# Leftover tokens of a top-1 MoE: the first gathered item as a ninth batch, the small item in column groups

## The chip, the cores and the metric

The kernel runs on one core of a Trainium2 chip. The metric is the device time of one execution in microseconds (us), as the median of several runs; every time below is in us unless ns is written. A core has five engines: TensorE (PE, with its weight loads shown apart as PEld), VectorE (DVE), ScalarE (ACT), GpSimd (POOL) and SyncE (SP, which here only issues DMA transfers and loads registers), and 16 DMA engines that serve all queues.

## What is computed

Sigmoid attention for 8 batches, 12 heads, 448 positions and 64 features a head feeds a mixture of 8 experts, of which each token takes one.

```python
def _attn_ref(q, k, v):
    scores = scale * np.matmul(q, k.transpose(0, 1, 3, 2)) - np.log(S)
    attn = 1.0 / (1.0 + np.exp(-scores))
    return np.matmul(attn, v)

def _moe_ref(x, w_gate, w1, w2):          # x 3584 x 768, w1 8 x 768 x 1024, w2 8 x 1024 x 768
    logits = x @ w_gate
    expert_idx = np.argmax(logits, axis=1)
    ...
    for e in range(E):
        xe = x[expert_idx == e]
        h = np.maximum(xe @ w1[e], 0.0)
        out[mask] = gate_w[mask, None] * (h @ w2[e])
```

On the inputs used, one expert holds nearly every token of a batch. What is left over, worked out from the reference, is 218 tokens of expert 7 and one token of expert 3.

## The kernel before

**Attention.** The 48 pairs of heads (g = 0 to 47, six for each batch) are read by SyncE and POOL: `load_pair` brings q and k, `load_values` (line 443, the transfer in 450) brings v. v of groups 4 to 9 comes through POOL's queue, all others through SyncE's (`V_POOL`, line 519). Scores (line 489) and weighted values (line 505) are plain fp32 matmuls on 64 by 64 tiles of the PE array; of every pair of such instructions one logical product is made.

**A batch of the MoE.** `moe` (line 194) runs for each batch the expert that most of its tokens chose, over all 448 tokens: layer 1 in line 210 (stationary: a 128 by 128 piece of w1), layer 2 in line 233. Each operand is split into a high and a low part in fp32r, and each product is made of three matmuls (high·high, high·low, low·high). `Weights` (line 135) feeds them: raw weights come by SyncE into a ring `wst` of five buffers (`load`), then ACT casts the high part (line 133) and POOL subtracts it for the low one (line 134), into rings of 3 buffers for w1 and 5 for w2 (`ahead`). The matmuls of attention and MoE are generators that are woven into each other; the order is written out by hand, and `until(n)` (line 626) lets the last batch run until n of its matmuls are left. A batch is written to the output by SyncE (line 190).

**The leftover.** Tokens that chose another expert than their batch's are noted as records (token, gate) in memory. They form items: each with one expert, and either up to 256 rows (large) or up to 128 rows (small). Counting and ordering them is done on DVE and POOL by lines 640 to 701, inside the last batch. Then two loops run with a number of passes that is only known at run time: the one of line 906 over the large items, the one of line 911 over the small. Here each is passed once. One pass, `item` (line 804), multiplies with the rows in the stationary place: 512 columns of w1 in layer 1, after which h is transposed (line 861) and split again, and 256 columns of w2 in layer 2 (all in line 815). Its positions of splits are the numbers in `AT`. `scatter` (line 768) writes the results of the item before, on POOL. The first item's rows are gathered by POOL (line 724) while the last batch runs, and its w1 is loaded and split then too (`w1h_item`, `w1l_item`).

Of the kernel before, what the change touches and what calls it, by code (L numbers as in the profile page):

```python
# [19 lines left out]
P = 128  # L20
# [5 lines left out]
def tile_sigmoid_attention_top1_moe(  # L26
# [109 lines left out]
    class Weights:  # L136
# [24 lines left out]
        def ahead(self, n):  # L161

            while True:
# [355 lines left out]
    WARM, FILL, V_POOL, K_POOL = 60, 20, 10, 12  # L519
# [90 lines left out]
    wts = Weights([(lambda b=b: regs.get(b)) for b in range(B)])  # L610
# [18 lines left out]
    for s, n in attention():  # L629
        if s >= START:  # L630
# [12 lines left out]
    AT = (  # L643
        (
            dict(zip((0, 1, 2, 3, 4, 12, 5, 6, 7, 8, 13, 14, 15, 16, 9, 10, 11, 17),
                     (38, 43, 48, 54, 60, 84, 102, 108, 114, 120, 126, 132, 138, 144, 150, 156, 162, 175))),
            (74, 90, 128, 168),
        ),
        (dict(zip((0, 1, 4, 5, 8, 9, 2, 3, 6, 7, 10, 11), (16, 20, 24, 28, 33, 42, 48, 54, 60, 66, 72, 78))), ()),
    )  # L650
    NK = NT // TL
    NI = E * NK


    xo = rest.tile([P, 2, DM], F32, name="xo")
    scr = xo.rearrange("p t f -> p (t f)")
# [8 lines left out]
    nc.gpsimd.iota(ek(1), pattern=[[NK, E], [1, NK]], base=0, channel_multiplier=0, allow_small_or_imprecise_dtypes=True)  # L665
# [5 lines left out]
    nc.vector.tensor_scalar(cut(0), cut(0), float(P), None, op0=ALU.add)  # L671
# [5 lines left out]
    ends = rest.tile([P, 2], F32, name="ends")  # L677
    nc.vector.tensor_copy(ends[:, 0:1], rank[0][:, NI - 1 : NI])
    nc.vector.tensor_add(ends[:, 1:2], ends[:, 0:1], rank[1][:, NI - 1 : NI])
    nc.vector.tensor_scalar(rank[1], rank[1], ends[:, 0:1], None, op0=ALU.add)  # L680
    for msk, cum in zip((big, few), rank):
        nc.vector.scalar_tensor_tensor(msk, cum, slot1, msk, op0=ALU.is_equal, op1=ALU.mult)
# [8 lines left out]

    ki = rest.tile([1, 2], I32, name="ki")
    nc.vector.tensor_scalar(ends[:, 0:1], ends[:, 1:2], -1.0, ends[:, 0:1], op0=ALU.add, op1=ALU.max)
# [6 lines left out]
    nc.vector.tensor_copy(li, pli[0:1, :TL])  # L700
    more(8)

    recs_v = recs.rearrange("(i t p) w -> i p t w", t=2, p=P)
    rec_s = rest.tile([P, 2, 2], U32, name="rec_s")
    rec_c = rest.tile([P, 2, 2], U32, name="rec_c")
    rec_n = rest.tile([P, 2, 2], U32, name="rec_n")
    xg = rest.tile([P, 2, DM], F32, name="xg")
    xp = xo.rearrange("p t (k f) -> p t k f", f=P)
# [3 lines left out]
    w1h = rest.tile([P, KD, DF], F32R, name="w1h_item")  # L712
    w1l = rest.tile([P, KD, DF], F32R, name="w1l_item")
# [7 lines left out]
    def get_rows(ireg, rec, nh):  # L721
        nc.sync.dma_start(rec, recs_v[bass.ds(ireg, 1)].rearrange("o p t w -> (o p) t w"))
        for t in range(nh):
            nc.gpsimd.indirect_dma_start(
                out=xg[:, t, :],
                out_offset=None,
                in_=x_tok,
                in_offset=bass.IndirectOffsetOnAxis(ap=rec[:, t, 0:1], axis=0),
                bounds_check=NT - 1,
                oob_is_err=False,  # L730
            )

    def sort_rows(nh):
        for t in range(nh):
            nc.vector.tensor_copy(
                xp[:, t].rearrange("p k (i s) -> p k i s", s=32), xg[:, t].rearrange("p (i k s) -> p k i s", i=4, s=32)
            )

    def split_rows(k2, nh):
        px = ps_x.tile([P, 512], F32, tag="px", name=f"px_{k2}")  # L740
        w = nh * P
        for kk in range(2):
            for t in range(nh):
                at = kk * w + t * P
                nc.tensor.transpose(px[:, at : at + P], xp[:, t, 2 * k2 + kk], ident)
        for kk in range(2):
            xh, xl = xrs[2 * k2 + kk]
            part = px[:, kk * w : (kk + 1) * w]
            nc.scalar.copy(xh[:, :w], part)
            nc.vector.tensor_sub(xl[:, :w], part, xh[:, :w].bitcast(F32))  # L750

    RAWS = [(wpool, "wst")] * RAWS_AHEAD
    turn = itertools.count()

    def raw_tile(name):
        pool, ring = RAWS[next(turn) % len(RAWS)]
        bufs = RAWS_AHEAD if ring == "wst" else None
        return pool.tile([P, 1024], F32, tag=ring, bufs=bufs, name=name)

    def w1_load(ereg, t):  # L760
        st = raw_tile(f"w1r_{t}")
        nc.sync.dma_start(st, w1[bass.ds(ereg, 1), t * P : (t + 1) * P, :].rearrange("e p n -> (e p) n"))
        return st

    def scatter(nh):
        puts = []
        for t in range(nh):
            put = nc.gpsimd.indirect_dma_start(
                out=out,
                out_offset=bass.IndirectOffsetOnAxis(ap=rec_s[:, t, 0:1], axis=0),  # L770
                in_=xo[:, t, :],
                in_offset=None,
                bounds_check=NT - 1,
                oob_is_err=False,
            )
            apart(put, puts)

    def no_rows():
        nc.gpsimd.iota(rec_s, pattern=[[0, 4]], base=int(BIG), channel_multiplier=0)

    no_rows()
    nc.gpsimd.memset(xg, 0.0)
    get_rows(item_reg(0), rec_c, 2)
    e0 = expert_reg(0)
    until(96)
    sort_rows(2)
    until(86)
    for k2 in range(KD // 2):
        split_rows(k2, 2)
        more(8)  # L790
    until(60)
    w1rs = [w1_load(e0, t) for t in range(3)]
    for t in range(KD):
        until(50 - 9 * t)
        part_split(w1rs[t], (w1h[:, t], w1l[:, t]), nc.vector)
        if t + 3 < KD:
            w1rs.append(w1_load(e0, t + 3))
    until(0)
    next(mo, None)
    order.close()  # L800
    RAWS = RAWS + [(hpool, f"hl{j}") for j in range(0, KF, 2)]
    ends_r = [nc.values_load(ki[0:1, a : a + 1], min_val=0, max_val=NI) for a in range(2)]

    def item(i, nh, split_at, sort_at):


        n = 0
        hooks = {}

        def at(m, f):  # L810
            hooks.setdefault(m, []).append(f)

        def mm(*a, **kw):
            nonlocal n
            nc.tensor.matmul(*a, **kw)  # L815
            n += 1
            for f in hooks.pop(n, ()):
                f()

        ereg = expert_reg(i)  # L820
        scatter(nh)
        if sort_at:
            enext = expert_reg(i + 1)
            get_rows(item_reg(i + 1), rec_n, nh)
        raws, parts = {}, {}
        todo = list(dict.fromkeys(u // 2 if u < NU else NU + u for u in split_at))

        def load():
            if todo:
                r = todo.pop(0)  # L830
                if r < NU:
                    raws[r] = raw_tile(f"w2r_{r}")
                    w2_rows(ereg, r, raws[r])
                else:
                    raws[r] = w1_load(enext, r - 2 * NU)

        def split(u):
            if u < NU:
                parts[u] = part_tiles("w2", 512, f"r_{u}")
                part_split(raws[u // 2][:, u % 2 * 512 : (u % 2 + 1) * 512], parts[u], nc.vector)  # L840
            else:
                t = u - NU
                part_split(raws[NU + u], (w1h[:, t], w1l[:, t]), nc.gpsimd if t % 2 else nc.vector)
            if u >= NU or u % 2:
                load()

        for _ in RAWS:
            load()
        for u, m in split_at.items():
            at(m, lambda u=u: split(u))  # L850
        half = DF // 2
        if sort_at:
            at(sort_at[0], lambda: sort_rows(nh))
            for k2 in range(KD // 2):
                at(sort_at[1 + k2], lambda k2=k2: split_rows(k2, nh))
        hts = {}

        def turn_h(f, h, hf):
            ph = ps_x.tile([P, 512], F32, tag="px", name=f"ph_{f}_{h}")
            for c in range(4):  # L860
# [81 lines left out]
```

## Time and profile before

| what | value |
| --- | --- |
| median of 3 runs | 869.01 (867.73 to 869.58) |
| the profiled execution: its own time | 869.31 |
| its span, from the first to the last instruction | 867.5 |
| granted clock of PE, mean | 0.993 |
| busy PE, ACT, POOL, DVE | 841.9 (97%), 388.8 (45%), 330.3 (38%), 318.1 (37%) |
| DMA | 120.61 MB, mean 139 GB/s |

The span is what the hardware profiler saw of one execution; about 1.8 of that execution's time lies outside it. Busy time of an engine is the time in which at least one of its instructions ran; PE's matmuls overlap, so their durations add up to more than the time they take, and what one costs is the distance to the next. "Idle before <- releaser" says what the engine waited for ahead of an instruction. The chain of waits goes back from the last instruction to what released it, step by step. The stretch to look at first is the end: the last batch's matmuls end near 793.9, the large item's near 838 and the small item's at 858.5.

### The profile page before, as it was taken

How to read it: one execution, taken by the hardware profiler on the slowest of the kernel's cores; microseconds unless marked ns; L12 is line 12 of the kernel's file. 1: busy time of each engine (PE TensorE's matmuls, PEld its weight loads, DVE VectorE, ACT ScalarE, POOL GpSimd, SP SyncE). 2: the span in 40 equal slices, each digit the busy share in tenths (PEclk: the TensorE clock that was granted, in tenths of full speed). 3: DMA queues.
4: the chain of work that ended last, by engine and by line, in shares of the span. 5: the costliest groups of instructions: out<-in, count | busy, mean ns of one | idle time of the engine just before them, and what ended most of it. 6: DMA issues, size and time to landing. Idle time of an engine off the chain costs nothing.

```text
span 867.5 us, 15542 instructions
## 1 busy us (share of the span) xinstructions
PE 841.9 (97%) x5642; PEld 640.1 (74%) x5642; DVE 318.1 (37%) x708; ACT 388.8 (45%) x697; POOL 330.3 (38%) x294
## 2 busy tenths in 40 slices
PE   8899999999999999999999999999999999999985
PEld 6464777777777767777777767777777789898875
DVE  2344135332363125322343134322352135435544
ACT  4567345345345445355345435255244422324533
POOL 8443332623243332624242413533242436641230
PEclk9999999999999999999999999999999999999998
DMA  9987764476556862786367753676454426545823
GB/s 152 127 177 188 168 156 91 97 183 159 102 128 140 190 142 51 169 187 149 70 144 176 166 123 80 149 166 146 88 151 108 118 65 165 157 111 152 287 73 111
DMA packets 326826, 120.61 MB, mean 139 GB/s; under 512 B 238596, under 2 KB 324052, under 8 KB 326752
## 3 DMA queue, kind: packets, MB, share of 16 engines
q1 hardware_dynamic: 320064, 113.77, 57.3%
q0 software_dynamic: 3904, 5.53, 3.0%
q8 instruction: 44, 0.72, 0.4%
q10 hardware_dynamic: 2784, 0.34, 0.4%
q14 instruction: 30, 0.25, 0.1%
HBM read 97.55 MB, written 24.64 MB: 141 GB/s over the span
## 4 chain that ended last, share of the span: by engine, by line
PE 88%; DMA 5%; SPq 2%; issue 2%; DVE 1%; ACT 1%; POOL 1%; POOLq 0%; another core or an unknown queue 0%; DVEq 0%; ACTq 0%
PE ps L233 26%; PE ps L210 26%; PE sc L489 14%; PE av L505 14%; PE ps L815 3%; PE psg L255 2%; DMA qn<-in_q_dram 2%; DMA w2r<-in_moe_w_dram 1%; SPq L437 1%; DMA vn<-in_v_dram 1%; DMA w1r<-in_moe_w_dram 1%; PE pg L372 1%; DVE w1l_item L134 1%; POOL w1l L134 0%; SPq L190 0%
## 5 line engine op out<-in xcount | busy, mean ns | idle before, releaser
L474 ACT ACTIVATE at<-sc,bias_s 128x448 f32<-128x448 f32 x336 | 188.1, 640 | 197.1 <-PE sc L489 188.8
L134 POOL TENSOR_TENSOR w2l<-wst,w2h 128x512 fp32r<-128x512 f32 x96 | 122.0, 1294 | 213.6 <-ACT w2h L133 213.5
L134 POOL TENSOR_TENSOR w1l<-wst,w1h 128x768 fp32r<-128x768 f32 x64 | 117.3, 1841 | 186.4 <-ACT w1h L133 166.3
L489 PE MATMUL sc<-qt,kt 64*64 64x448 f32 x1344 | 158.8, 547 | 3.8 <-DVE qt L458 2.1
L505 PE MATMUL av<-at,vn 64*64 64x448 f32 x1344 | 156.6, 543 | 3.8 <-DMA vn<-in_v_dram 3.8
L233 PE MATMUL ps<-hl,w2h 128*128 128x448 f32 x384 | 142.1, 370 | 0.0
L210 PE MATMUL ps<-xh,w1l 128*128 128x448 f32 x384 | 141.2, 368 | 0.8 <-POOL w1l L134 0.8
L210 PE MATMUL ps<-xh,w1h 128*128 128x448 f32 x384 | 141.3, 368 | 0.0
L210 PE MATMUL ps<-xl,w1h 128*128 128x448 f32 x384 | 141.2, 368 | 0.0
L233 PE MATMUL ps<-hh,w2h 128*128 128x448 f32 x384 | 141.1, 367 | 0.0
L233 PE MATMUL ps<-hh,w2l 128*128 128x448 f32 x384 | 140.8, 367 | 0.0
L489 PEld LDWEIGHTS sc<-qt,kt 64*64 64x64 f32 x1344 | 77.9, 191 | 62.6 <-issue 47.6
L218 DVE SCALAR_TENSOR_TENSOR hl<-ps,hh 128x448 fp32r<-128x448 f32 x64 | 40.0, 624 | 185.2 <-ACT hh L217 185.0
L505 PEld LDWEIGHTS av<-at,vn 64*64 64x64 f32 x1344 | 56.0, 133 | 67.1 <-issue 57.6
L217 ACT ACTIVATE hh<-ps 128x448 fp32r<-128x448 f32 x64 | 35.1, 549 | 137.2 <-PE ps L210 137.2
L133 ACT CAST w2h<-wst 128x512 fp32r<-128x512 f32 x96 | 57.7, 624 | 76.5 <-PE ps L233 74.9
L210 PEld LDWEIGHTS ps<-xh,w1l 128*128 128x128 f32 x384 | 72.1, 188 | 11.6 <-issue 4.6
L233 PEld LDWEIGHTS ps<-hl,w2h 128*128 128x128 f32 x384 | 74.6, 194 | 7.8 <-issue 3.9
L210 PEld LDWEIGHTS ps<-xl,w1h 128*128 128x128 f32 x384 | 72.1, 188 | 10.9 <-issue 4.9
L210 PEld LDWEIGHTS ps<-xh,w1h 128*128 128x128 f32 x384 | 72.1, 188 | 10.5 <-issue 4.8
L233 PEld LDWEIGHTS ps<-hh,w2h 128*128 128x128 f32 x384 | 74.6, 194 | 3.8
L233 PEld LDWEIGHTS ps<-hh,w2l 128*128 128x128 f32 x384 | 74.6, 194 | 3.4
(140 smaller groups left out, 759.2 us busy)
## 6 DMA issues: line engine op xcount, KB each, us to landing
wst<-in_moe_w_dram SPq DMA_DIRECT2D x64, 384.0 KB
wst<-in_moe_w_dram SPq DMA_DIRECT2D x48, 512.0 KB
x_tok<-xt SPq DMA_DIRECT2D x64, 168.0 KB
out_dram<-ob SPq DMA_DIRECT2D x96, 112.0 KB
qn<-in_q_dram SPq DMA_DIRECT2D x186, 56.0 KB
vn<-in_v_dram SPq DMA_DIRECT2D x84, 112.0 KB
kn<-in_k_dram SPq DMA_DIRECT2D x148, 56.0 KB
w1r<-in_moe_w_dram SPq DMA_DIRECT2D x12, 512.0 KB
```

The costliest lines, as they stand in the source:

```text
L133: nc.scalar.copy(hi, st)
L134: eng.tensor_tensor(lo, st, hi.bitcast(F32), op=ALU.subtract)
L210: nc.tensor.matmul(ps[:, :S], a[:, ws], b_, start=(t == 0 and n == 0), stop=(t == KD - 1 and n == 2))
L217: nc.scalar.activation(hh[:, :S], ps[:, :S], AF.Relu)
L218: nc.vector.scalar_tensor_tensor(hl[:, :S], ps[:, :S], 0.0, hh[:, :S].bitcast(F32), op0=ALU.max, op1=ALU.subtract)
L233: nc.tensor.matmul(ps[:, :S], a, b_, start=(j == 0 and n == 0), stop=(j == KF - 1 and n == 2))
L255: nc.tensor.matmul(psg[: 2 * E, :S], wgs[:, t], xch[b, t][n], start=(t == 0 and n == 0), stop=(t == KD - 1 and n == 1),)
L372: nc.tensor.transpose(pg[:, c * P : (c + 1) * P], gates[:, b, c : c + 1].broadcast_to([P, P]), ident)
L474: nc.scalar.activation(at, ps[:, :S], AF.Sigmoid, bias=bias_s, scale=SCALE)
L489: nc.tensor.matmul(ps[quarter(g, h), :S], ks, ops[g, "q"][OWN[h]], start=True, stop=True)
L505: nc.tensor.matmul(psv[g][OWN[h], :S], ops[g, "v"][rows, c, :], at[rows], start=(c == 0), stop=(c == KC - 1))
L815: nc.tensor.matmul(*a, **kw)
```

## The change

1. **v on SyncE.** `V_POOL` is gone; `load_values` uses SyncE for all groups.
2. **The first item is a ninth batch.** It always runs, as a large one. `large(wts, B)` takes its expert as the ninth entry of `Weights`, so that its weights pass through the same rings as those of the batches. In layer 1 a piece of w1 is stationary and the 256 rows move (h comes out turned the right way), in layer 2 h is stationary and 256 columns of w2 move: 144 and 144 matmuls, each of 256 columns. The rows are sorted and turned as before, at places before and in the last batch. Its results go to buffers of the output ring `ob` and are scattered at the end. `wts.low` moves the low parts of w2 from POOL to DVE from the last 50 matmuls of the last batch on.
3. **Small items have up to 32 rows** (`TS`), down from 128, and are computed in plain fp32, without splitting. `small_item` puts the 32 columns of output on one of four column groups of the array (`GRP`), adds up the four by a matmul with `fold` (four identities below one another), and does so in both layers. One such item (the second in the order of items) is woven into the ninth batch, in six pieces after matmuls 20, 36, 60, 78, 156 and 176 (`TINY`); its 14 weight pieces are loaded by SyncE, one at a time, from when 130 matmuls of the last batch are left.
4. **The loops** are still there for more items, from the second large one and from the second small one on: on these inputs neither has a pass.

The names stay; the line numbers move. The core of the diff:

```diff
@@ Weights
+        low = nc.gpsimd
...
-                    part_split(st[:, u % 2 * 512 : (u % 2 + 1) * 512], parts, nc.gpsimd)
+                    part_split(st[:, u % 2 * 512 : (u % 2 + 1) * 512], parts, self.low)
@@ load_values
-        eng = nc.sync if g < 4 or g >= V_POOL else nc.gpsimd
...
-            eng.dma_start(t[quarter(g, h)], v[b, 2 * hp + h].rearrange("(p c) d -> p c d", c=KC))
+            nc.sync.dma_start(t[quarter(g, h)], v[b, 2 * hp + h].rearrange("(p c) d -> p c d", c=KC))
@@ the batches
-    wts = Weights([(lambda b=b: regs.get(b)) for b in range(B)])
+    wts = Weights([(lambda b=b: regs.get(b)) for b in range(B + 1)])
...
-    ps_m2 = ctx.enter_context(tc.tile_pool(name="ps_m2", bufs=3, space=bass.MemoryType.PSUM))
+    ps_m2 = ctx.enter_context(tc.tile_pool(name="ps_m2", bufs=4, space=bass.MemoryType.PSUM))
@@ the items
+    def large(wts, b):
+        w0 = b * wts.PARTS
+        hts = []
+        for j in range(KF):
+            wts.ahead(w0 + (3, 4, 5, 6, 7, 9, 11, 13)[j])
+            whi, wlo = wts.parts.pop(w0 + j)
+            ps = ps_moe.tile([P, 512], F32, tag="moe", name=f"psi1_{j}")[:, :TL]
+            for t in range(KD):
+                xh, xl = xrs[t]
+                ws = slice(t * P, (t + 1) * P)
+                for n, (a, b_) in enumerate(((whi, xh), (whi, xl), (wlo, xh))):
+                    nc.tensor.matmul(ps, a[:, ws], b_, start=(t == 0 and n == 0), stop=(t == KD - 1 and n == 2))
+                    yield
...
+            nc.scalar.activation(hh, ps, AF.Relu)
+            nc.vector.scalar_tensor_tensor(hl, ps, 0.0, hh.bitcast(F32), op0=ALU.max, op1=ALU.subtract)
...
+        for d in range(ND):
+            for h in range(2):
+                ps = ps_m2.tile([P, 512], F32, tag="m2", name=f"psi2_{d}_{h}")[:, :DW]
+                for j in range(KF):
...
+                    for n, (a, b_) in enumerate(((hh, whi), (hh, wlo), (hl, whi))):
+                        nc.tensor.matmul(ps, a, b_, start=(j == 0 and n == 0), stop=(j == KF - 1 and n == 2))
+                        yield
+                    if h == 1 and j % 2:
+                        wts.ahead(w0 + KF + min(NU, 4 * d + j // 2 + 6))
+                to, gate = xo[h][:, d * DW : (d + 1) * DW], rec[:, h, 1:2].bitcast(F32)
+                nc.vector.tensor_scalar(to, ps, gate, None, op0=ALU.mult)
...
+        for h in range(2):
+            apart(scatter(xo[h], rec[:, h, 0:1]), puts)
+    GRP = [slice(c * TS, (c + 1) * TS) for c in range(4)]
+    def small_item():
+        xs = hpool.tile([P, 1024], F32, tag="hh6", name="xs")[:TS, :DM]
+        sort_rows(xs, xgs)
+        yield
...
+        for t in range(KD):
+            nc.tensor.transpose(px[:, t * TS : (t + 1) * TS], xs[:, t * P : (t + 1) * P], ident[:TS, :TS])
...
+        for n in range(2 * KD):
+            f, t = divmod(n, KD)
+            nc.tensor.matmul(
+                pss[f][GRP[n % 4], :half], xts_s[:, t * TS : (t + 1) * TS], w1s[:, t, f * half : (f + 1) * half],
+                start=(t < 4), stop=(t + 4 >= KD),
+            )
...
+        for j in range(KF):
+            nc.tensor.matmul(ph[:, j * TS : (j + 1) * TS], hp[:, j * P : (j + 1) * P], fold, start=True, stop=True)
...
+        for j in range(KF):
+            for ps, cs in zip(pss, cols):
+                nc.tensor.matmul(
+                    ps[GRP[j % 4], : cs.stop - cs.start], ht[:, j * TS : (j + 1) * TS], w2s[:, j, cs],
+                    start=(j < 4), stop=(j >= KF - 4),
+                )
...
+            nc.tensor.matmul(pf[:TS, : cs.stop - cs.start], fold, op[:, cs], start=True, stop=True)
...
+        scatter(xo[:TS, :DM], rec_s[:, 0, 0:1])
@@ the end of the program
+    get_rows(item_reg(0))
+    regs[B] = expert_reg(0)
+    first = nc.sync.value_load(ki[0:1, 0:1], min_val=1, max_val=NI)
+    small_rows(item_reg(first))
+    e_s = expert_reg(first)
...
+    for n in range(130, 90, -10):
+        until(n)
+        load_some(1)
+    xp = sort_large()
     for k2 in range(KD // 2):
-        split_rows(k2, 2)
-        more(8)
+        split_rows(xp, k2)
+        until(82 - 8 * k2)
+        load_some(1)
+    until(50)
+    wts.low = nc.vector
+    for n in range(40, -1, -10):
+        until(n)
+        load_some(1)
...
+    TINY = (20, 36, 60, 78, 156, 176)
+    for n, _ in enumerate(large(wts, B)):
+        if n % 12 == 6:
+            load_some(1)
+        if n in TINY:
+            next(tiny)
...
-    with tc.For_i(0, ends_r[0]) as i, tc.manual_schedule():
-        item(i, 2, *AT[0])
-    with tc.manual_schedule():
-        scatter(2)
-        no_rows()
-    with tc.For_i(ends_r[0], ends_r[1]) as i, tc.manual_schedule():
-        item(i, 1, *AT[1])
-    scatter(1)
+    with tc.For_i(1, counts[0]) as i, tc.manual_schedule():
...
+    with tc.For_i(counts[1], counts[2]) as i, tc.manual_schedule():
...
```

Three places show what moves. The first is SyncE's queue near the start of the program (vn, qn and kn are v, q and k of one group; x_tok is the copy of the tokens in memory). Before:

```order
L450 DMA vn_368<-in_v_dram 64x448 x2
L437 DMA qn_406<-in_q_dram 32x14x32 x4
L437 DMA qn_492<-in_q_dram 32x14x32 x4
L437 DMA qn_567<-in_q_dram 32x14x32 x4
L396 DMA x_tok<-xt_0_427 32x14x96 x4
```

With the change:

```order
L450 DMA vn_368<-in_v_dram 64x448 x2
L438 DMA qn_406<-in_q_dram 32x14x32 x4
L450 DMA vn_452<-in_v_dram 64x448 x2
L438 DMA qn_492<-in_q_dram 32x14x32 x4
L450 DMA vn_499<-in_v_dram 64x448 x2
L438 DMA qn_567<-in_q_dram 32x14x32 x4
L450 DMA vn_574<-in_v_dram 64x448 x2
L397 DMA x_tok<-xt_0_427 32x14x96 x4
```

After v of group 3 (vn_368) each q is followed by the v of a group that POOL used to issue. The second place is POOL in layer 1 of the last batch, where the item's rows are gathered (xg the large item's rows, xgs the small one's; w1l_6 is the low part of the batch's seventh piece of w1). Before:

```order
L134 TENSOR_TENSOR w1l_5_7986<-wst_5_7758,w1h_5_7985 128x768
L779 IOTA rec_s 128x4
L782 MEMSET xg 128x1536
L724 DMA xg<-x_tok,rec_c 128x768 x2
L134 TENSOR_TENSOR w1l_6_8063<-wst_6_7812,w1h_6_8062 128x768
```

With the change:

```order
L133 TENSOR_TENSOR w1l_5_7992<-wst_5_7758,w1h_5_7991 128x768
L866 MEMSET xg 128x1536
L867 MEMSET xgs 32x768
L717 DMA xg<-x_tok,rec 128x768 x2
L717 DMA xgs<-x_tok,rec_s 32x768
L133 TENSOR_TENSOR w1l_6_8097<-wst_6_7812,w1h_6_8096 128x768
```

A third gather stands ahead of the sixth low part. The third place is PE at the small item. Before, it has a loop of its own:

```order
L802 TENSOR_LOAD ki
L911 COMPARE_AND_BRANCH
L911 UNCONDITIONAL_BRANCH x2
L937 BRANCH_PREFETCH_HINT
L815 MATMUL ps_0_0_8972<-w1h_item,rxh_8015 128x512
```

With the change, its pieces stand between matmuls of the large item (psi_3, line 776); this is layer 1, the third piece:

```order
L776 MATMUL psi_3_8587<-rxh_8024,w1h_3_8516 128x256
L830 MATMUL pss_0_8595<-w1s,xts_s 32x512 x6
L830 MATMUL pss_1_8596<-w1s,xts_s 32x512 x6
L776 MATMUL psi_3_8587<-rxl_8025,w1h_3_8516 128x256
L776 MATMUL psi_3_8587<-rxh_8024,w1l_3_8517 128x256
```

The twelve fp32 matmuls of 512 columns go to the four column groups in turn, and the large item goes on behind them.

## Rows read from the trace of the kernel before

**Rows 1.** The page, part 4: the chain that ended last, by engine and line

```profile
PE ps L233 26%; PE ps L210 26%; PE sc L489 14%; PE av L505 14%; PE ps L815 3%; PE psg L255 2%; DMA qn<-in_q_dram 2%; DMA w2r<-in_moe_w_dram 1%; SPq L437 1%; DMA vn<-in_v_dram 1%; DMA w1r<-in_moe_w_dram 1%; PE pg L372 1%; DVE w1l_item L134 1
```

**Rows 2.** By stretch: us, PE PEld DVE ACT POOL busy, PEclk, DMA share, GB/s

```profile
767.30:793.90 26.60, 26.60 (x137) 25.24 (x137) 16.29 (x23) 11.34 (x18) 9.16 (x7) 1.00 0.50 148
793.90:838.00 44.10, 40.26 (x255) 35.49 (x253) 22.80 (x35) 20.48 (x35) 11.53 (x7) 0.96 0.49 158
838.00:858.50 20.50, 18.43 (x118) 16.28 (x116) 9.92 (x19) 9.52 (x17) 3.14 (x4) 1.00 0.58 187
858.50:867.50 9.00, 0.00 (x0) 0.00 (x0) 0.55 (x2) 0.00 (x0) 0.98 (x1) 0.74 0.01 2
```

**Rows 3.** The chain of waits at the head: start, us, what

```profile
23.07 6.41 DMA vn<-in_v_dram
```

**Rows 4.** The timeline of POOL and of SyncE, 22 to 27: start, us

```profile
24.22 1.08 POOL L450 DMA_DIRECT2D vn<-in_v_dram  x2 [0.94 <-PE sc L489]
...
24.47 2.53 SPq L437 DMA_DIRECT2D qn<-in_q_dram  x3
```

**Rows 5.** The timeline of POOL and PE, 747 to 757, [idle <-releaser]

```profile
751.81 1.08 POOL L724 DMA_INDIRECT xg<-x_tok,rec_c  x1 [3.93 <-DMA rec_c<-recs]
753.19 1.03 POOL L724 DMA_INDIRECT xg<-x_tok,rec_c  x1 [0.30 <-issue]
...
756.14 0.47 PE L210 MATMUL ps<-xh,w1l 128*128 128x448 f32 x1 [0.81 <-POOL w1l L134]
```

**Rows 6.** The chain of waits, 798 to 806: register loads on SyncE

```profile
801.99 0.38 SPq L719
...
802.79 0.27 SPq L719
```

**Rows 7.** The chain of waits in the second half of the items

```profile
830.10 0.69 DVE w2l_r L134
...
850.90 7.56 PE ps L815 x63
```

**Rows 8.** The groups by form, 793.9 to 837.9, line 815 on PE

```profile
L815 PE MATMUL ps<-w2l_r,h 128*128 128x256 f32 x48 | 14.3, 299 | 1.8 <-DVE w2l_r L134 1.8
```

**Rows 9.** Everything on the raw weights wst: ns minimum, median, maximum

```profile
L134 POOL TENSOR_TENSOR w2l<-wst,w2h x96: 1267/1292/1598, 112.0 to 784.5; 128x512 fp32r<-128x512 f32 x96
...
L133 ACT CAST w1h<-wst x64: 824/827/882, 75.3 to 751.8; 128x768 fp32r<-128x768 f32 x64
L134 POOL TENSOR_TENSOR w1l<-wst,w1h x64: 1812/1846/1868, 78.4 to 756.0; 128x768 fp32r<-128x768 f32 x64
```

**Rows 10.** Fp32 tiles: a page group, and the chain of waits

```profile
L489 PE MATMUL sc<-qt,kt 64*64 64x448 f32 x1344 | 158.8, 547 | 3.8 <-DVE qt L458 2.1
...
179.72 1.50 PE sc L489 x16
...
224.98 1.67 PE av L505 x16
```

**Rows 11.** The timeline of PE, 744 to 746

```profile
744.41 0.60 PE L698 MATMUL pli<-ident,lf 128*1 128x128 f32 x4
744.93 0.47 PE L210 MATMUL ps<-xh,w1h 128*128 128x448 f32 x1
```

**Rows 12.** The timeline of POOL, 857 to 862

```profile
860.14 0.98 POOL L768 DMA_INDIRECT out_dram<-xo,rec_s  x1 [9.55 <-issue]
```

**Rows 13.** Line 937: ns minimum/median/maximum, first and last start

```profile
L937 POOLq DRAIN  x3: 46/110/6757, 859.9 to 867.2; - x3
```

**Rows 14.** The timeline of PE, 838.0 to 840.5

```profile
839.81 0.49 PE L815 MATMUL ps<-w1h_item,rxh 128*128 128x512 f32 x1 [1.74 <-issue]
```

**Rows 15.** The chain of waits, 740 to 760: the record load

```profile
747.73 3.26 DMA rec_c<-recs
```

**Rows 16.** The page, part 2: all packets

```profile
DMA packets 326826, 120.61 MB, mean 139 GB/s; under 512 B 238596, under 2 KB 324052, under 8 KB 326752
```

**Rows 17.** The DMA view, 812 to 820

```profile
DMA packets 1765, 3.04 MB, mean 380 GB/s; under 512 B 255, under 2 KB 1280, under 8 KB 1765
```

More of the change, by code (lines that the diff above doesn't have):

```diff
@@ L690, in tile_sigmoid_attention_top1_moe @@
     nc.vector.tensor_reduce(lf, prod, axis=AX.X, op=ALU.add)
-    ki = rest.tile([1, 2], I32, name="ki")
-    nc.vector.tensor_scalar(ends[:, 0:1], ends[:, 1:2], -1.0, ends[:, 0:1], op0=ALU.add, op1=ALU.max)
+    nc.vector.tensor_scalar(lf[:, 0:1], lf[:, 0:1], float(NONE), None, op0=ALU.add)
+    ki = rest.tile([1, 3], I32, name="ki")
     nc.vector.tensor_copy(ki, ends[0:1])
@@ L700, in tile_sigmoid_attention_top1_moe @@
     nc.vector.tensor_copy(li, pli[0:1, :TL])
+    nc.vector.tensor_reduce(fold, ident.rearrange("p (c m) -> p m c", m=TS), axis=AX.X, op=ALU.add)
     more(8)
     recs_v = recs.rearrange("(i t p) w -> i p t w", t=2, p=P)
[L704 to L708, printed above, removed]
+    recs_s = recs.rearrange("(i r) w -> i r w", r=TL)
+    rec = rest.tile([P, 2, 2], U32, name="rec")
+    rec_s = rest.tile([TS, 1, 2], U32, name="rec_s")
     xrs = [
@@ L733, in sort_rows, with gather @@
[L733 to L739, printed above, removed]
+    def gather(to, idx):
+        nc.gpsimd.indirect_dma_start(
+            out=to,
+            out_offset=None,
+            in_=x_tok,
+            in_offset=bass.IndirectOffsetOnAxis(ap=idx, axis=0),
+            bounds_check=NT - 1,
+            oob_is_err=False,
+        )
@@ new lines, in scatter, with get_rows, sort_rows @@
+    def scatter(frm, idx):
+        return nc.gpsimd.indirect_dma_start(
+            out=out,
+            out_offset=bass.IndirectOffsetOnAxis(ap=idx, axis=0),
+            in_=frm,
+            in_offset=None,
+            bounds_check=NT - 1,
+            oob_is_err=False,
+        )
+    def get_rows(ireg):
+        nc.sync.dma_start(rec, recs_v[bass.ds(ireg, 1)].rearrange("o p t w -> (o p) t w"))
+        for t in range(2):
+            gather(xg[:, t, :], rec[:, t, 0:1])
+    def sort_rows(to, frm):
+        nc.vector.tensor_copy(
+            to.rearrange("p (k i s) -> p k i s", i=4, s=32), frm.rearrange("p (i k s) -> p k i s", i=4, s=32)
+        )
@@ L746, in split_rows @@
         for kk in range(2):
             xh, xl = xrs[2 * k2 + kk]
[L748 to L765, printed above, removed]
-        puts = []
[L767 to L774, printed above, removed]
-            )
-            apart(put, puts)
@@ new lines, in tile_sigmoid_attention_top1_moe @@
+    until(50)
[3 more added lines that the diff above has]
+        load_some(1)
+    next(mo, None)
+    tiny = small_item()
+    TINY = (20, 36, 60, 78, 156, 176)
[4 more added lines that the diff above has]
+            next(tiny)
+    order.close()
+    counts = [nc.values_load(ki[0:1, a : a + 1], min_val=1, max_val=NI) for a in range(3)]
+    with tc.For_i(1, counts[0]) as i, tc.manual_schedule():
+        ereg = expert_reg(i)
+        get_rows(item_reg(i))
+        xp = sort_large()
+        for k2 in range(KD // 2):
+            split_rows(xp, k2)
+        for _ in large(Weights([lambda: ereg]), 0):
+            pass
@@ L917 @@
+    with tc.For_i(counts[1], counts[2]) as i, tc.manual_schedule():
+        ereg = expert_reg(i)
+        small_rows(item_reg(i))
+        for n in range(KD + KF):
+            small_load(ereg, n)
+        for _ in small_item():
+            pass
 _INS = ["q", "k", "v", "moe_w_gate", "moe_w1", "moe_w2"]
```

217 lines of the change are left out of this document (78 added, 139 removed).

## The prediction, made before the changed kernel ran

> **What bounds the kernel now.** I read the chain of waits by line first [rows 1]: it is TensorE (PE) almost everywhere, so cheaper work on PE, or a PE wait taken away, shortens the run as long as nothing else comes last. The table by stretch [rows 2] shows where PE is not full. In the first row (last batch) its 26.60 us are all busy. The large item takes 44.10 us with PE busy for 40.26, and even that holds transposes and warm-up matmuls. The small item takes 20.50 us. In the last 9.00 us PE does nothing. What can be won lies in these last 73.6 us; the batches before them are the same in both kernels, apart from two places (head and gather, below). The profiled execution took 869.31 us, 1.8 more than its span of 867.5; the median of the three runs is 869.01, 0.3 lower. I sum against 869.31.
>
> **1. Head: six v loads go from POOL to SyncE.** v of group 3 is issued at 23.07 and lands 6.41 later [rows 3]; PE waits for it. Meanwhile POOL issues another v pair at 24.22 [rows 4], whose transfer competes. It now stands behind q of three more groups on SyncE, where the order above puts it. I take −0.5. The rows can't give the share that the competitor costs, so the bounds are −1.3 (a fifth of the 6.41) and +2 (if a later v comes so late that PE waits: the three q issues that follow on SyncE take 2.53 [rows 4], less some slack).
>
> **2. The third gather, on POOL.** Today two gathers stand ahead of the last two low-part subtractions of w1, and PE waits 0.81 for the first of these [rows 5]. The gathers start 1.38 apart. A third stands there now, and its record load comes after three more register loads on SyncE, of some 0.8 each (801.99 to 802.79) [rows 6], which run beside the first two gathers' wait. So the subtraction is one spacing later: **+1.3**; bounds 0 (if PE's other work slides in) and +3.7 (record load not hidden: three times 0.8 more).
>
> **3. The large item, as a ninth batch.** Both kernels multiply 256 rows: today 72 matmuls of 512 columns and 144 of 256, then 288 of 256 columns, the same columns. 63 matmuls of 256 take 7.56 us [rows 7], 0.120 each, so 288 take 34.6. The rest of today's 44.1 is waiting and side work: 1.8 us for w2l_r [rows 8], transposes, hand-over of h through ACT and VectorE (DVE), warm-up. The new order has none of it, if its weights are ready. Layer 1 takes 18 × 0.120 = 2.16 us of PE for each 128 columns; their split is a cast on ACT, 0.83, and a subtraction on POOL, 1.85 [rows 9], below 2.16, and ACT and POOL work on different parts. A layer 2 part feeds 12 matmuls in 1.44, the POOL price is 1.29 [rows 9], and the change gives these to DVE, which did one in 0.69 [rows 7]. So the splits are the cover and PE the bound: 34.6 − 44.1 = **−9.5**; bounds −9.5 and −5.5 (late parts, about 0.3 for each of 12).
>
> **4. The small item, in column groups.** 20.5 us of separate item go away. Its row is now worked on in pieces between the large item's matmuls, which cost PE their own time:
> - 6 transposes: four records of 128 columns cost 0.52 (744.41 to 744.93) [rows 11], 0.13 each. Six are 0.8 at that price, 0.2 by their 32 columns; I take 0.6.
> - Layer 1, 12 matmuls of 512 columns in fp32, spread over four column tiles. The trace has fp32 on 64 by 64 tiles: 1344 records of 547 ns in 158.8 us of busy time, so four run at a time [rows 10]. 16 records (eight matmuls of 448 columns, two records each) take 1.50: 1.67 ns a column and tile. 12 × 512 × 1.67 / 4 = 2.57.
> - 8 folding matmuls with 32 columns: 16 records are 2.1 at the same price [rows 11] and 0.5 by columns. I take 1.4.
> - Layer 2, 8 × 768 columns on four tiles: 2.57. The last fold, 768 columns on one tile: 768 × 1.67 = 1.28.
> - Eight changes of tile shape: the first row of 16 after a full-size matmul takes 1.67, not 1.50 [rows 10], so 0.15 each, 1.2.
>
> Together 9.6, so **−10.9**. Bounds of the piece time: 7.2 (no cost of changing, folds by columns) and 25.1 (if column groups run one after another: 10.3 instead of 2.57, twice). I take four at a time because the 64 by 64 tiles do so.
> The Trainium skill, TensorE: Matmul & The Clock Gate, in Part 3, § Measured speedup vs the span model, gives three column tiles of 32, with 512 to stream, 2.38 times the speed of one, not three. By that the two layers would cost 2.57 × 3 / 2.38 = 3.24 each, and the sum would be 1.3 more (an estimate from that page). No run here shows 32-wide tiles yet.
>
> **5. The end.** From PE's last matmul (858.5) to the end of the span are 9.0 us today [rows 2]: DVE 0.5, a POOL scatter of 0.98 [rows 12], its landing, for which POOL's drain lasts until 866.7 [rows 13], and the final barrier. What is new: both loops are now crossed without a pass, after the scatters. Today's way from one loop to the next lets PE idle for 1.74 [rows 14]. Two crossings are 3.5. Each also jumps over a whole loop body; no row prices that. It lies between 0 and the 3.26 of the small transfer of the records [rows 15], should the target have to be fetched; I take 0.85. Sum 5.2. The two scatters: the first can go while PE still works, the second is the one of today, some 0.6 earlier, and the last piece of the small item is long done. The order holds the landing ahead of the jumps (the jump's rows wait for the DMA queues), so I add in full, and subtract 1.0 for DVE and the record copies that disappear: **+4.2**; bounds −1.0 (all of it beside the landing) and +9.0 (two jumps at 3.26).
>
> **Sum:** −0.5 + 1.3 − 9.5 − 10.9 + 4.2 = −15.4: 853.9 against the profiled 869.31, **853.6** against the median.
>
> **The rivals.**
> *Column groups run one after another* (12%). For it: no row has 32-wide tiles, and the groups share rows of the array. Against: [rows 10]. Price: 2 × 7.7 = 15.4, which takes back the whole gain: 869.0, on either side of today.
> *Jumps that fetch* (14%). Each jump over a loop body costs as much as the transfer of the records, 3.26 [rows 15], not 0.85: +4.8, 858.4. For it: a loop body holds hundreds of instructions, and the engine stands on its far side after the jump. Against: nothing but the absence of a row. The Trainium skill, Runtime: NRT & Kernel Launch, § Instruction fetch mechanics, speaks for it: a taken branch whose target is outside the fetched window waits for a DMA fetch of the target's page. No jump over a loop body was taken in this trace, so no row shows it.
> *Weights too late for the ninth batch* (10%). It needs the ring of raw weights, in which nothing is free until a split has read it; now all of it goes through one ring of five while SyncE also issues 14 loads for the small item and twelve stores. For it: today PE waits 1.8 for a split in the item [rows 8]. If layer 1 is paced by ACT plus POOL in series (0.83 + 1.85 = 2.68, not 2.16, for eight parts) and layer 2 loses 0.2 on each of 12 parts: +6.6, about 860.
> *The DMA can't bring it all* (8%): the slower end. From about 765 on SyncE has to move 14 pieces for the ninth batch and 14 for the small item (of 384 and 512 KB), 13,632 KB with twelve stores of 112 KB (14.0 MB). At the run's mean of 139 GB/s [rows 16] that is 100 us: the last piece at 865, then 6 us of matmuls and the end of 13 to 14: 885. It decides when the rate stays under about 165 GB/s (landing after 849). Against: 380 GB/s from 812 to 820 [rows 17]; at 300 it takes 47 us.
> *The change doesn't do what it says*: if the leftover of the small expert were over 32 rows, it would pass through the loop as a large item. On these inputs one expert has 218 leftover rows and another has one (worked out from the reference), and the stretches of the trace hold one passage of each loop [rows 2], so this has no chance of its own.
>
> **How the numbers follow.** The forecast has 56%: 853.6. The jumps that fetch (858.4) and the late weights (860.2) lie above it; below it −2.4 from folds and changes of tile (the 7.2 of part 4) and −3 from a cheaper end (part of the way to its lower bound): 848. Upward, late weights and part of the +4 of late parts: 864. The range, 848 to 864, leaves out the serial groups and the DMA, 20%. A run can be told from no change beyond 0.2%, 1.7 us. Faster: the forecast 0.56, jumps 0.14, late weights 0.10, and a quarter of the serial case 0.03: 0.83. Same: half of the serial case, 0.06. Slower: a quarter of it and the DMA: 0.11.
>
> **What would show it.** Right: 288 matmuls of the large item 0.12 apart, with no idle time ahead of them but where pieces stand; each of the small item's layers in 2.6 us (24 and 32 records); PE's wait ahead of w1l near 757 up from 0.8 to about 2.1; PE's last matmul near 839; some 13 us from there to the end of the span; the last of the small item's weights landing well before the piece that reads it. Wrong: a layer of the small item of 5 us or more; idle time of PE that ends with wst or w1l in the large item; an end that stays at 9 us or goes beyond 18; or a PE wait for v in the head.

## The result, and the profile after

The changed kernel takes 857.86 us as the median of four runs (856.05 to 859.16); the kernel before took 869.3 beside it. The ratio is 0.9865, with a 95% interval of 0.9841 to 0.9888. A second set of runs, on which the experiments below stand, gave 856.11 against 866.13, ratio 0.9873 (0.9852 to 0.9893). So the change is worth 10 to 11.4 us. The forecast was 853.6 with a range of 848 to 864; the measured time lies inside the range, and the gain that was forecast, 15.4, is a third more than the 11.4 measured beside it.

The profiled execution took 859.16 (span 857.3) against 869.31 (span 867.5): −10.15. The table by stretch answers to [rows 2]; its columns are the same. The first stretch ends where the large item starts, the second at PE's last matmul.

```profile
765.00:797.40 32.40, 32.40 (x166) 30.70 (x165) 10.31 (x19) 9.25 (x17) 17.17 (x13) 1.00 0.83 256
797.40:842.00 44.60, 44.59 (x371) 39.05 (x369) 18.54 (x32) 15.38 (x29) 11.12 (x7) 1.00 0.47 147
842.00:857.30 15.30, 0.00 (x0) 0.00 (x0) 0.48 (x1) 0.00 (x0) 0.98 (x1) 0.65 0.10 35
```

The large item with the small one inside it takes 44.60, all of it busy, where the two took 64.6 (793.9 to 858.5). The end has grown from 9.0 to 15.3. And the large item starts 3.5 later than before, at 797.40 instead of 793.9: something was lost ahead of it. PE's longest waits, over the whole span (us in total, times, longest):

```profile
PE av L505 <- DMA vn<-in_v_dram: 3.7, 1, 3.7
PE sc L489 <- ACT at L474: 1.8, 2, 1.3
PE ps L211 <- POOL w1l L133: 1.7, 1, 1.7
PE sc L489 <- DVE qt L458: 1.6, 3, 0.9
```

The first row is as long in the kernel before:

```profile
PE av L505 <- DMA vn<-in_v_dram: 3.8, 1, 3.8
```

The second row lies in the head, with its 1.3 at 79.67. The third is the wait behind the gathers, 0.81 before [rows 5]. No row names a split of the ninth batch. In the PE timeline, where the third piece stands, the next matmul of the large item comes right behind it:

```profile
805.27 0.28 PE L776 MATMUL psi<-rxh,w1h 128*128 128x256 f32 x1
...
805.48 2.78 PE L830 MATMUL pss<-w1s,xts_s 128*32 128x512 f32 x24
808.19 0.39 PE L776 MATMUL psi<-rxl,w1h 128*128 128x256 f32 x1
```

The matmuls stand 0.12 apart, and the twelve fp32 matmuls (24 records) add 808.19 − 805.27 − 0.12 = 2.80, and 0.10 more at the next distance.

### The profile page after: what moved, and what is told of

It reads as the page before. It is cut to its first block, busy times and chain, and to the rows that moved or that the text cites. A ratio compares the mean times of both kernels' runs of the same rounds, so it can differ in the third digit from the quotient of the medians.

```text
span 857.3 us, 15476 instructions
## 1 busy us (share of the span) xinstructions
PE 830.9 (97%) x5642; PEld 630.1 (74%) x5642; DVE 297.9 (35%) x685; ACT 371.6 (43%) x672; POOL 327.2 (38%) x282
## 5 line engine op out<-in xcount | busy, mean ns | idle before, releaser
L133 POOL TENSOR_TENSOR w1l<-wst,w1h 128x768 fp32r<-128x768 f32 x72 | 131.9, 1841 | 201.6 <-ACT w1h L132 179.6
L505 PE MATMUL av<-at,vn 64*64 64x448 f32 x1344 | 158.9, 542 | 3.7 <-DMA vn<-in_v_dram 3.7
L132 ACT CAST w2h<-wst 128x512 fp32r<-128x512 f32 x108 | 65.0, 623 | 83.5 <-PE ps L234 75.2
L211 PEld LDWEIGHTS ps<-xl,w1h 128*128 128x128 f32 x384 | 72.1, 188 | 10.9 <-issue 4.9
```

Source lines behind the costliest of these rows:

```text
L132: nc.scalar.copy(hi, st)
L133: eng.tensor_tensor(lo, st, hi.bitcast(F32), op=ALU.subtract)
L211: nc.tensor.matmul(ps[:, :S], a[:, ws], b_, start=(t == 0 and n == 0), stop=(t == KD - 1 and n == 2))
L505: nc.tensor.matmul(psv[g][OWN[h], :S], ops[g, "v"][rows, c, :], at[rows], start=(c == 0), stop=(c == KC - 1))
```

## The experiments

The changed kernel is the starting point of each. "The end" is the time from the end of PE's last matmul to the end of the span, and "the item" the time from the start of the large item's first matmul to that of its last. The kernel before ran beside all of them.

**The yardstick.** No edit.

> The changed kernel once more, as the yardstick for the others of this call. First theory (the 3 us between its runs, 856.05 to 859.16, are waits that fall differently from run to run): a median of 856.5 to 858.5. Rival (the runs came in two groups, near 856.4 and near 859.1, for a reason that lies in the chip and not in the order): again only values near one of the two.

Measured: 856.11 (853.75 to 856.75), item 44.31, end 15.65. The item is the same to the hundredth; what differs between executions lies elsewhere. The median lies just below what the first theory gave. The runs do not fall on the two values that the rival names, as one of them took 853.75; with the first set they spread over 5 us.

**The head.**

```diff
+        eng = nc.sync if g < 4 or g >= 10 else nc.gpsimd
...
-            nc.sync.dma_start(t[quarter(g, h)], v[b, 2 * hp + h].rearrange("(p c) d -> p c d", c=KC))
+            eng.dma_start(t[quarter(g, h)], v[b, 2 * hp + h].rearrange("(p c) d -> p c d", c=KC))
```

> The changed kernel with v of groups 4 to 9 on POOL again. First theory (v behind q on SyncE comes late; it is the 1.05 that PE has lost by 64.64 us and the 1.25 by 110.45, against the kernel before): PE reaches score matmul number 336 at 110.4 to 110.7, not 111.70, and the time falls by about 1.2. Rival (the head's time lies in other moved instructions, or is noise between executions): 111.5 or more, and no change of the time.

Measured: 856.02 (ratio 0.9884, 0.9866 to 0.9902): no difference to the yardstick. PE reaches score matmul number 336 (counted from 0, two records to each product) at 109.72. That would speak for the first theory, had the other kernels, all with v on SyncE, not reached it at 108.31 to 111.70 (eleven executions, mean 109.90). The spread of the same head is 3.4 us, more than the move can be worth. What the first profile showed as a loss of 1.25 is a draw from it. The first theory falls; so does the rival's 111.5, while its reading as noise holds. PE's wait for v in the head, the one that step 1 of the prediction set out from, is here

```profile
PE av L506 <- DMA vn<-in_v_dram: 3.4, 1, 3.4
```

and so no longer than the 3.7 of the changed kernel, where the pair that was said to compete with that v is issued later.

**The end without loops.**

```diff
-    counts = [nc.values_load(ki[0:1, a : a + 1], min_val=1, max_val=NI) for a in range(3)]
-
-    with tc.For_i(1, counts[0]) as i, tc.manual_schedule():
...
-    with tc.For_i(counts[1], counts[2]) as i, tc.manual_schedule():
...
```

> The changed kernel without its two loops and the three register loads for them: the items beyond the first two, of which these inputs have none, are left out. First theory (crossing two loops that are not passed costs 8.0 us between the last scatter, 843.77, and POOL's final drain, 851.79, and the drain lasts 4.6 by itself): from PE's last matmul to the end of the span 7 to 8 us instead of 15.3, and a time lower by 7.5 to 8. Rival (the crossing covers the landing of the scatters, and without it the drain grows to the 6.8 of the kernel before): 9 to 9.5 us from PE's end to the end of the span, a time lower by some 6. Second rival (the jumps lie beside the landing and cost little): lower by under 2.

Measured: 846.36 (ratio 0.977, 0.9757 to 0.9784), end 7.25 instead of 15.65 (15.28 in the first profile). The crossing costs 8.0 to 8.4, and the first theory's end holds; both rivals fall. The time fell by 9.8, more than that theory gave. Between the two profiled executions (856.21 and 845.78) most of what the end leaves over is a quicker head (110.88 and 108.92). POOL's final drain, in the answers on the program's last line (ns minimum/median/maximum, first and last start), here

```profile
L924 POOLq DRAIN  x3: 46/109/5863, 837.0 to 843.4; - x3
```

and in the changed kernel

```profile
L941 POOLq DRAIN  x3: 46/109/4638, 851.8 to 857.0; - x3
```

differ by the last scatter (0.98, started 0.24 after the drain's), which the first contains: 5.86 − 1.21 = 4.65 behind the scatter, with its landing, and 4.64 after the crossing too, where the drain starts 8 us behind the end of the scatter and 4.8 after its last piece has landed (847.0). So the 4.6 are not the landing.

**One loop only.** The second loop is left out.

```diff
-    with tc.For_i(counts[1], counts[2]) as i, tc.manual_schedule():
...
```

> The changed kernel without its second loop (the small items beyond the first, of which these inputs have none, are left out); the first loop and all three register loads stay. First theory (each crossing has its own price; both together took 8.3 of PE's end to the span's end, 15.5 against 7.2 without loops): 11 to 12 us from PE's last matmul to the end of the span, a ratio to the kernel before of 0.981 to 0.984. Rival (most of the price is paid once, for the first barrier and PE's jump): 13.5 or more, a ratio above 0.985.

Measured: 851.14 (ratio 0.982, 0.9798 to 0.9842), end 10.30, below what either theory gave; the ratio is the first theory's. Each crossing has a price, but not the same: the first 3.05 (10.30 − 7.25), the second 5.0 to 5.35 (15.28 and 15.65, less 10.30). PE's branches and POOL's drain in this kernel, from the lines of the loop and of the program's end:

```profile
L903 PEldq COMPARE_BRANCH  x3: 97/295/3670, 837.5 to 847.6; - x3
```

```profile
L934 POOLq DRAIN  x3: 50/109/4638, 843.9 to 849.1; - x3
```

PE's jump takes 3.67 and PE is not through the loop before 847.6, while POOL has been in its drain since 843.9: the drain covers PE's lateness. The changed kernel shows what a second loop adds, first PE's and POOL's branches of its first loop:

```profile
L903 PEldq COMPARE_BRANCH  x3: 104/292/3309, 841.5 to 850.0; - x3
L903 POOLq COMPARE_BRANCH  x3: 33/38/49, 844.0 to 848.0; - x3
```

then the register loads and the second loop:

```profile
L901 POOLq TENSOR_LOAD <-ki x3: 293/308/511, 843.4 to 848.5; - x3
L911 PEldq COMPARE_BRANCH  x3: 82/176/194, 851.4 to 853.2; - x3
L911 POOLq INC_SWDGE_SEM  x1: 1270/1270/1270, 849.1 to 849.1; - x1
L911 POOLq EVENT_SEMAPHORE  x13: 17/43/85, 849.0 to 851.5; - x13
```

POOL leaves the first loop at 848.0 and starts its drain at 851.8. It fills these 3.8 us itself: two register loads from 848.1 to 848.8, INC_SWDGE_SEM (an instruction that POOL runs once in each loop's barrier) from 849.1 to 850.35, then a row of semaphore checks. PE is at the second branch at 851.4, close behind, but POOL hardly waits for it: the longest of POOL's 13 semaphore rows there is 0.085 us, in the yardstick 0.38. In the run with v on POOL none is over 0.043, and its end is no shorter (15.9, of which 0.6 is a longer drain). So the second crossing is dear by POOL's own work, not by a wait for PE. The other 1.3 of its price lie at the first loop, where POOL's last branch comes 6.0 after PE's last matmul here and 4.7 without the second loop. The edit also takes the two register loads away: they are for the second loop's bounds, and POOL has one load of that line there instead of three. How the price divides between loads, INC_SWDGE_SEM and checks was not tried.

**One jump over both loops.**

```diff
+    with tc.If(counts[2] > 2):
-    with tc.For_i(1, counts[0]) as i, tc.manual_schedule():
+        with tc.For_i(1, counts[0]) as i, tc.manual_schedule():
...
-    with tc.For_i(counts[1], counts[2]) as i, tc.manual_schedule():
+        with tc.For_i(counts[1], counts[2]) as i, tc.manual_schedule():
...
```

> The changed kernel with both loops inside one condition on the count (more than two items), so that on these inputs one jump goes over both bodies instead of one over each; nothing is left out. First theory (each crossing costs its own barrier and its own jump, about half of the 8.0 us): lower by 3.5 to 4.5. Rival (the jump is fetched over a distance, and one long jump costs what two shorter ones do): lower by under 1.

Measured: 849.85 (ratio 0.981, 0.9792 to 0.9828), end 10.9: the end is shorter by 4.7, a little more than the first theory gave, the time by 6.3. The rival falls. PE's jump over both bodies took 3.68, over one 3.27 to 3.77.

**The third gather.**

```diff
-    small_rows(item_reg(first))
+    nc.sync.dma_start(rec_s, recs_s[bass.ds(item_reg(first), 1), 0:TS].rearrange("o r (t w) -> (o r) t w", t=1))
...
         until(n)
+        if n == 120:
+            gather(xgs, rec_s[:, 0, 0:1])
         load_some(1)
```

> The changed kernel with the third gather (the small item's row) moved on POOL from ahead of the last two low parts of w1 to the point where 120 matmuls of the last batch are left; its record load stays where it is. First theory (the third gather holds up w1l by one spacing of 1.3): PE's wait for w1l near 757 falls from 1.70 to 0.8 or less, and the time by about 0.9, near what a comparison of runs can tell. Rival (the wait is set by the record load and the register loads ahead of it, not by the number of gathers): the wait stays at 1.5 or more, and so does the time.

Measured: 854.03 (ratio 0.9864, 0.9835 to 0.9892). PE's wait is 0.73:

```profile
754.22 0.47 PE L211 MATMUL ps<-xh,w1l 128*128 128x448 f32 x1 [0.73 <-POOL w1l L133]
```

It was 1.70 and 2.2 in the two executions of the changed kernel, and 1.6 to 2.4 in the eight other runs with the gather in its old place. The number of gathers sets it, and the first theory holds for the wait: the kernel without loops has all three gathers in the old place but none of the three register loads, and PE waits 1.8. The intervals of the ratios overlap, so the 1 us is shown by the wait, not by the time.

**One column group.**

```diff
-                pss[f][GRP[n % 4], :half], ...
-                start=(t < 4), stop=(t + 4 >= KD),
+                pss[f][GRP[0], :half], ...
+                start=(t == 0), stop=(t == KD - 1),
...
-                    ps[GRP[j % 4], : cs.stop - cs.start], ...
+                    ps[GRP[0], : cs.stop - cs.start], ...
```

> The changed kernel with all matmuls of the small item's two layers on one column group instead of four in turn (the folds then add one group). First theory (four column groups run at the same time): the pieces of layer 1 and layer 2, 2.90 and 2.94 in the changed kernel, become 10.3 to 10.6 each, and the time rises by 15 to 15.5. Rival (the groups run one after another anyway, and the pieces are short for another reason): the pieces and the time stay as they are.

Measured: 870.65, ratio 1.0048 (1.0031 to 1.0065), slower than the kernel before by half a per cent, and 14.5 above the yardstick (15 to 15.5 were expected). Layer 1 of the small item in the PE timeline:

```profile
801.54 10.49 PE L830 MATMUL pss<-w1s,xts_s 128*32 128x512 f32 x24
```

10.49 on one group, 2.78 on four: 3.77 times. The item takes 60.00 instead of 44.31. The column groups are what makes the small item cheap inside the large one; without them the change would lose.

**No pieces.**

```diff
-        if n in TINY:
-            next(tiny)
```

> The changed kernel without the small item's six pieces (sorting, transposing, multiplying and scattering its one row are left out; its loads and its gather stay). First theory (the pieces stand on PE's path with all that they cost): the large item takes 34.5 to 34.6 from its first to its last matmul instead of 44.4, and the time falls by 9.5 to 10.5. Rival (the pieces fill time in which PE would wait for splits of the ninth batch's weights): it falls by less than 7, and PE shows waits for w1l or w2l.

Measured: 844.4, ratio 0.9756 (0.9722 to 0.979); the item takes 34.43. So the pieces cost 44.31 − 34.43 = 9.9 of PE's time, and they hide no wait: without them there is none either. The time fell by 11.7, more than expected, 1.2 of it at the end (14.4).

**Low parts of w2 on POOL.**

```diff
-    wts.low = nc.vector
```

> The changed kernel with the low parts of the ninth batch's w2 left on POOL. First theory (a part feeds 12 matmuls in 1.44 us, and POOL needs 1.29, so POOL just keeps up and DVE was not needed): the large item stays at 44.3 to 45 us from its first to its last matmul, and the time within 1 us of the changed kernel. Rival (POOL's scatter of the small item, 0.94, and layer 1's subtractions ahead of it make it late): PE shows waits for w2l of 2 us or more, and the item takes 46 or more.

Measured: 856.05, as the yardstick (ratio 0.9876, 0.9851 to 0.9901); the item takes 45.33, 1.0 more, with these waits of PE:

```profile
PE psi L793 <- POOL w2l L133: 0.5, 2, 0.3
```

POOL keeps up, with 1 us lost on the way: just outside what the first theory gave, far from the rival.

**No last scatter.** Without loops, and without the large item's two scatters.

```diff
-        puts = []
-        for h in range(2):
-            apart(scatter(xo[h], rec[:, h, 0:1]), puts)
```

> The changed kernel without its two loops and without the two scatters of the large item (its rows of the output are not written; the items beyond the first two are left out). First theory (POOL's final drain takes some 4.6 from the end of POOL's own last transfer, which is now the small item's scatter, 10 us before PE's end, and so lies beside PE's work): 1.5 to 2.5 us from PE's last matmul to the end of the span, against 7.2 with the scatters. Rival (the drain costs its 4.6 wherever it starts, and starts when the other engines are done): 5.5 to 6.5.

Measured: 840.3, ratio 0.9691 (0.9666 to 0.9717), end 1.5. The drain is as long as ever, but lies beside the matmuls:

```profile
L921 POOLq DRAIN  x3: 46/109/5658, 823.9 to 837.9; - x3
```

It starts at 823.9, has the small item's scatter (824.17, 0.93) in it, and is over at 829.6, 4.5 behind that scatter and 7 ahead of PE's end. So it counts from POOL's own last transfer, not from the end of the others.

**A version that beats both.** One condition around the loops, only its own register load ahead of it, and the gather moved.

```diff
-    counts = [nc.values_load(ki[0:1, a : a + 1], min_val=1, max_val=NI) for a in range(3)]
+    total = nc.values_load(ki[0:1, 2:3], min_val=1, max_val=NI)
...
+    with tc.If(total > 2):
+        counts = [nc.values_load(ki[0:1, a : a + 1], min_val=1, max_val=NI) for a in range(2)] + [total]
...
```

> A version meant to beat both kernels, with nothing left out: the two loops inside one condition, of the three register loads only the one for the condition ahead of it, and the third gather moved as in the run before. First theory (what is left of the crossing is one barrier, one jump and one register load on POOL's path, and the gather is worth 0.9): 10.0 or less from PE's last matmul to the end of the span, against 10.9 with the condition alone, and 847 to 849 for the time, as a ratio to the kernel before 0.978 to 0.981. Rival (PE's jump of 3.7 sets the end, not POOL's register loads): 10.7 or more for the end, a ratio above 0.981.

Measured: 847.99 (846.06 to 848.45), ratio 0.979 (0.9764 to 0.9817), end 9.8; PE's wait for w1l is 0.4. That is faster than the changed kernel (0.9873, 0.9852 to 0.9893); from the run with the condition alone (0.981, 0.9792 to 0.9828) the times do not tell it apart, only the end and the wait do, in one execution each. The two rows of its end, line of the condition and last line:

```profile
L905 PEldq COMPARE_BRANCH  x1: 4065/4065/4065, 833.8 to 833.8; - x1
```

```profile
L945 POOLq DRAIN  x3: 46/109/4636, 838.8 to 844.0; - x3
```

PE's jump is over at 837.9 and POOL starts its drain at 838.8, so POOL's chain of scatter, register load and barrier sets the end, not PE's jump, even at 4.07. This jump too goes over both bodies.

## Why the prediction was right, and where a term was wrong

In the terms of the sum, for the profiled executions:

| term | predicted | measured | in the yardstick |
| --- | --- | --- | --- |
| 1. head, by score matmul 336 | −0.5 | +1.25 | +0.43 |
| other drift, up to the last score matmul | 0 | +1.35 | −1.49 |
| 2. third gather, up to the large item | +1.3 | +0.89 | +1.23 |
| 3 and 4. both items, first to last start | −20.4 | −19.95 (64.26 to 44.31) | −19.95 |
| 5. the end | +4.2 | +6.22 | +6.59 |
| sum | −15.4 | −10.2 | −13.2 |

Of the 5.2 us between sum and measurement in the first profile, 3.1 are head and drift, and they are chance: in the yardstick the two came out 0.6 below the forecast. What both executions have in common is step 5, 2.0 and 2.4 above its term.

**Steps 3 and 4 held.** The large item alone takes 34.43 (34.6 predicted), the pieces together 9.9 (9.6): 0.67 for the transposes, 2.90 and 2.94 for the layers, 1.79 for the folds, 1.60 for the last fold, each with the 0.08 to 0.10 that the following matmul is late. The trace of before had no 32-wide tile, and the price taken from 64 by 64 tiles [rows 10], 1.67 ns a column and tile, was near: 2.78 against 2.57. One thing step 3 did not see: the 44.1 of the old large item, which it split into matmuls, waiting and side work, hold 3.4 us at the lower of the clock's two levels, 1.2 GHz (granted clock 0.72 in 830 to 836, after PE had been busy 5.06 of the 6 us before); the new item has 1.00 throughout. What this cost was not tried. Of the rivals, *column groups one after another* falls by the run on one group, *weights too late* by the absence of any PE wait in the ninth batch. *The DMA can't bring it all* falls too: SyncE issued the last of the small item's loads at 804.5, and 17 us later its layer 2 began; the weights came at 256 GB/s from 765 to 797.4, where the rival needed less than 165.
The Trainium skill, TensorE: Matmul & The Clock Gate, Part 3, § Measured speedup vs the span model, has 2.38 for three column tiles; the prediction's estimate from it was 3.24 for each layer. The trace has 2.80 and 2.84 (2.90 and 2.94 with the late matmul behind), and 3.77 times for four tiles. The measurement decides.

**Step 5 was right in its direction and wrong in its size and its path.** It read POOL's drain as the landing of the last scatter, and priced two crossings at 5.2 by PE: twice the 1.74 that PE had idled between the loops, and 0.85 for each jump, which no row gave. The drain is 4.64 whether or not a transfer is left to land. The end without loops is 7.25, 1.8 below before (predicted: 1.0 below). The two crossings then cost 8.0, not 5.2, and by the rows of the changed kernel it is POOL that pays them, with register loads, INC_SWDGE_SEM, semaphore checks and, at the first loop, a wait of 0.7 for the scatter's landing. The jump on PE takes 3.3 to 4.1, so *jumps that fetch* named the right price of a jump (3.26). But the jump lies beside POOL's work: at the second loop's barrier POOL waits for PE under 0.1 in the first profile, 0.4 in the yardstick, and at most 0.6 in any run. That this rival's 858.4 is nearest to the measured time is luck, by the head and drift above.
The Trainium skill, Runtime: NRT & Kernel Launch, § Instruction fetch mechanics, lets a taken branch outside the fetched window wait for its page. The trace agrees. The DMA view of the changed kernel, from 842.2 to 845.5, has a row of a queue of the kind `instruction` beside that of the scatter (packets, MB, share of 16 engines):

```profile
q8 instruction: 1, 0.02, 1.8%
```

This packet of 16 KB runs from 843.17 to 844.12, inside PE's jump (842.18 to 845.49). All ten traces with a long jump have one such packet in it, and in all ten the jump ends 1.35 to 1.39 after the packet, though the jumps last from 3.27 to 4.07. Without loops there is no such row between PE's last matmul and the end. No run kept the jump and took the fetch away.

**Step 1 can't be told from nothing.** The time of the head shows neither sign: the run with v back on POOL made no difference in time, and one head varies by 3.4 us. Its mechanism has no support: PE's wait for v is 3.8 before, 3.7 with the change and 3.4 with v back on POOL. The drift of +1.35 between head and last score matmul was no term of the sum. It is made of steps of 0.1 to 1.0 in attention, the largest (1.0) near 652, where no row of PE shows a wait. The stretch takes 573.25 in the kernel before, 574.60 here and 571.76 in the yardstick, so two executions of one kernel differ by 2.8: chance, too.

**Step 2 held**, +0.9 and +1.2 for +1.3: PE's wait for w1l grew from 0.81 to 1.70, and to 2.2 in the yardstick. A gather still costs its spacing of 1.3; where PE itself comes later than the gathers do, it waits less.

## What to carry to other kernels

A few rows that need the same kind of work need not be a stage of their own: in pieces inside a full stage, in column groups, they cost PE little more than their columns in the layers (2.78 for 2.57), though more in the small steps around them (1.79 for the folds, 0.5 by columns), and the waits of a stage of its own disappear. A loop that is passed zero times is not free: here two of them cost 8 us behind the last matmul, most of it on POOL; one condition around both takes back more than half, and with the loads for bodies that are not entered inside it the end went from 10.9 to 9.8. Before a term of some 1 us is predicted from two profiles, look at how much the same place varies between executions.

## What was not expected of the hardware

- POOL's final drain takes 4.64 us after a crossing, 8 us behind its last scatter (5.2 in the run with v on POOL), and 4.65 from the end of a scatter right behind its start (5.55 in the kernel before); when POOL's last transfer came early, the drain ran beside PE's work and the end shrank to 1.5.
- PE's jump over a loop body takes 3.3 to 3.8 us, over two bodies 3.68 and 4.07, and ends 1.35 to 1.39 after a 16 KB packet of the instruction queue; the branches of the other four engines took no more than 0.07 each in their own rows.
- Four 128 by 32 column tiles in fp32 run 3.77 times as fast as one.
